# Products of loaded tiles by themselves in TensorE's waits, from Sinkhorn to v of batch 1

## The chip, the core and the metric

The kernel runs on one core of one Trainium2 chip. Its engines work side by side, each through its own list of instructions in order: TensorE (PE; its weight loads are listed as PEld), VectorE (DVE), ScalarE (ACT), GpSimd (POOL) and SyncE (SP), which here only issues DMAs. Sixteen DMA engines move data. The metric is the device time of one execution in microseconds (us); the profile comes from one further execution of the same program.

## What is computed

Sinkhorn attention over four batches of eight heads, 768 positions and 64 channels, followed by a token and channel mixer. Cut to what matters:

```python
# attention; q, k, v: (4, 8, 768, 64); sort_net: (4, 8, 8, 8)
P = sort_net
for _ in range(5):
    P = P - max(P, -1); P = exp(P)
    P = P / (sum(P, -1) + 1e-9)
    P = P / (sum(P, -2) + 1e-9)
k_sorted = einsum('bhij,bhjcd->bhicd', P, k_blocks)   # 8 blocks of 96 positions
v_sorted = einsum('bhij,bhjcd->bhicd', P, v_blocks)
attn = softmax(q_block @ k_sorted_block.T / 8)        # block by block
x = (attn @ v_sorted_block), heads beside each other: (4, 768, 512)
# mixer
u  = x + lam * einsum('ts,bsd->btd', w_tok, alpha1 * x + beta1)
a2 = alpha2 * u + beta2
out = u + lam * (relu(a2 @ w_ch1) @ w_ch2)            # 512 -> 2048 -> 512
```

## The kernel before

The order of the work is written out by hand: each engine gets its instructions in the order in which the Python code issues them, and the tile framework adds the semaphore waits. PSUM is held in two pools of two buffers each (`psS`, `psM`); `ps2` takes the next buffer of a pool, two banks of 512 columns.

The first 60 us, which the change touches, run in this order on TensorE.

1. While q and k of batch 0 arrive through GpSimd's DMA queue, 60 products of a column of ones by itself (L730) write to the tile `spare`. `sinkhorn` runs its five turns on VectorE and ScalarE with two yields a turn; between them `q_path(0)` transposes q of batch 0 on TensorE (L409) and ScalarE copies the result (L418).
2. `big_p("k")` spreads P over 128 partitions by a product (L258) and three VectorE operations (the last, L270, makes PTk). `mix_k(0)` mixes k of batch 0: three rounds of 64 small products (L309), each round into one buffer of each pool and copied out by ScalarE and VectorE (L294). `big_p(0)` does the same for v of batches 0 and 1.
3. `scores_max(0)` has eight steps, each with eight products (L447) and one maximum on VectorE (L453); between them go the eight steps of `mix_v(0)`, v of batch 0, each with eight products (L359) and a copy on ScalarE (L367).
4. `tok_weights` transposes w_tok (L685, six groups of six; copies L689, most of them on ScalarE), three groups ahead of `heads(0)` and three behind it. `heads(0)` computes, in eight steps, scores less their maxima (L490, L498), exponentials on ScalarE (L505), the products with v (L515) and the division on VectorE (L524, L525). After steps 4 and 8, `bounce` writes four blocks of x to DRAM on SyncE's queue (L535); at the end `read(0)` reads the first half back, on ScalarE's queue (L543), and `read(1)` the second, on SyncE's.
5. `row_sums` multiplies w_tok by ones (36 products of one column, L698), `big_p(1)` spreads P for batches 2 and 3, `mix_v(1)` makes v of batch 1 (L359, copies in turn on ScalarE and VectorE), with three VectorE additions (`add_x0`, L573) in between, and `mix_k(1)` mixes k of batch 1.
6. `mixing()` starts with `tok_mix(0)`: per group of 128 tokens, six products of 128x128 by 512 columns (L586). From there on the mixer's products (L586, L642, L664) and the attention of batches 1 to 3 are issued in turn by costs that the code counts.

GpSimd's queue loads, in order, q, k and v of batch 0, w_tok, v and k of batch 1, the small vectors, q of batch 1 and the first half of w_ch1 (W1); the second half of W1 and w_ch2 follow only when a copy on GpSimd (L778) has seen the second half of x of batch 0 read back.

Of the kernel before, what the change touches and what calls it, by code (L numbers as in the profile page):

```python
# [19 lines left out]
def kernel(  # L20
# [18 lines left out]
    nc = tc.nc  # L39
# [48 lines left out]
    raw_of = {}  # L88
# [194 lines left out]
            )  # L283


    kT_of, vS_of = {}, {}

    def kT_tile(b):
# [7 lines left out]
    def mix_k(b):  # L296

        raw, PK = raw_of["k", b], PT_of["k"]
        kT_tile(b)
        for rnd in range(3):  # L300
            ps = ps2(psM), ps2(psS)
            for turn in range(2):
                for tt in range(8):
                    for th in range(2):
                        for hl in range(2):
                            bank = (hl + turn) % 2
                            t = rnd * 16 + bank * 8 + tt
                            r = slice(th * 64 + hl * 32, th * 64 + hl * 32 + 32)
                            nc.tensor.matmul(  # L309
                                ps[th][hl * 64:hl * 64 + 64, bank, tt * 32:(tt + 1) * 32],  # L310
                                raw[r, t * D:(t + 1) * D], PK[r, b, hl * 32:hl * 32 + 32],
                                start=True, stop=True,
                            )
            for th in range(2):
                cols = ps[th][:, :, 0:256].rearrange("p b (t c) -> p c b t", c=32)
                evict_k(
                    b, cols, th * (BLK // 2) + rnd * 16,
                    nc.vector.tensor_copy if th else nc.scalar.copy,
                )
            yield 2.4  # L320
# [33 lines left out]
    def mix_v(b, pool):  # L354
        r = slice(b * 64, b * 64 + 64)
        for d8 in range(D // 8):
            ps = ps2(pool)
            for dd in range(8):
                nc.tensor.matmul(  # L359
                    ps[:, 0, dd * 64:(dd + 1) * 64],  # L360
                    v01[r].rearrange("p (t d) -> p d t", d=D)[:, d8 * 8 + dd, :],
                    PT_of[0][r, r], start=True, stop=True,
                )
            dst = vS_of[b][:, :, d8 * 8:(d8 + 1) * 8]
            src = ps[0:BLK, 0].rearrange("p (d c) -> p c d", c=64)
            if b == 0 or d8 % 2 == 0:
                nc.scalar.copy(dst, src)  # L367
            else:
                nc.vector.tensor_copy(dst, src)
            yield 1.1  # L370
# [66 lines left out]
    def scores_max(b):  # L437

        mx = at([BLK, 2, H4, NB], FT, "mx", 1)
        for n in range(2 * H4):  # L440
            h4, g = divmod(n, 2)
            sp = ps2(psS)
            for i1 in range(4):
                i = g * 4 + i1
                for hl in range(2):
                    r = slice(hl * 64, hl * 64 + 64)
                    nc.tensor.matmul(  # L447
                        sp[0:BLK, hl, i1 * BLK:(i1 + 1) * BLK],
                        qT_of[b, h4][r, i * BLK:(i + 1) * BLK],
                        kT_of[b][r, h4 * 8 + i, :],  # L450
                        start=True, stop=True,
                    )
            nc.vector.tensor_reduce(  # L453
                mx[:, :, h4, g * 4:(g + 1) * 4],
                sp[0:BLK, :, 0:4 * BLK].rearrange("p l (i t) -> p l i t", t=BLK),
                AXX, ALU.max,
            )
            yield 1.0


        mh = at([BLK, 2, 2, H4 * NB], BF, "mh", 1)
        mxf = mx[:].rearrange("p l h i -> p l (h i)")
        nc.vector.tensor_copy(mh[:, :, 0, :], mxf)
        nc.vector.tensor_tensor(mh[:, :, 1, :], mxf, mh[:, :, 0, :], ALU.subtract)
        yield END
        tp = psS.tile([128, 2, 1024], BF, name="m_ps", tag="psS")
        nc.tensor.transpose(
            tp[:, 0, 0:BLK], mh[:].rearrange("p l e c -> p (l e c)"), identbf[0:BLK, 0:BLK]
        )
        for g in range(2):  # L470
            Dt = D_of[b, g] = at([128, 4, BLK], BF, "Dt", 2)
            nc.vector.tensor_tensor(
                Dt[:], tp[:, 0, 0:BLK].unsqueeze(1).to_broadcast([128, 4, BLK]),
                mask_j[:, g * 4:(g + 1) * 4].unsqueeze(2).to_broadcast([128, 4, BLK]), ALU.mult,
            )
        yield END
# [3 lines left out]
    def heads(b, xpool):  # L480

        xnat = at([BLK, NB, C], F16, "xnat", 1)
        ETs = {}

        def scores(n):
            g, h4 = divmod(n, H4)
            sp = ps2(psS)
            for hl in range(2):
                r = slice(hl * 64, hl * 64 + 64)
                nc.tensor.matmul(  # L490
                    sp[0:BLK, hl, 0:4 * BLK], nsel[r, h4, :], D_of[b, g][r],
                    start=True, stop=False, skip_group_check=True,
                )
            for i1 in range(4):
                i = g * 4 + i1
                for hl in range(2):
                    r = slice(hl * 64, hl * 64 + 64)
                    nc.tensor.matmul(  # L498
                        sp[0:BLK, hl, i1 * BLK:(i1 + 1) * BLK],
                        kT_of[b][r, h4 * 8 + i, :],  # L500
                        qT_of[b, h4][r, i * BLK:(i + 1) * BLK],
                        start=False, stop=(i1 == 3), skip_group_check=True,
                    )
            ET = ETs[n] = at([BLK, 2, 4, BLK], F16, "ET", 3)
            nc.scalar.activation(  # L505
                ET[:].rearrange("p l i s -> p l (i s)"), sp[0:BLK, :, 0:4 * BLK],
                AF.Exp, scale=scale,
            )

        def values(n):  # L510
            g, h4 = divmod(n, H4)
            xp = ps2(xpool)
            for hl in range(2):
                for i1 in range(4):
                    nc.tensor.matmul(  # L515
                        xp[0:BLK, hl, i1 * VP:i1 * VP + D + 1],
                        ETs[n][:, hl, i1, :],
                        vS_of[b][:, hl * 32 + h4 * 8 + g * 4 + i1, 0:D + 1],
                        start=True, stop=True,
                    )  # L520
            xg = xp[0:BLK, :, 0:4 * VP].rearrange("p l (i e) -> p l i e", e=VP)
            recip = at([BLK, 2, 4], FT, "recip", 2)

            nc.vector.reciprocal(recip[:], xg[:, :, :, D])  # L524
            nc.vector.tensor_tensor(  # L525
                xnat[:, g * 4:(g + 1) * 4, :].rearrange(
                    "p i (l h d) -> p l i h d", l=2, d=D
                )[:, :, :, h4, :],
                xg[:, :, :, 0:D],
                recip[:].unsqueeze(3).to_broadcast([BLK, 2, 4, D]), ALU.mult,  # L530
            )

        def bounce(g):
            for i in range(g * 4, g * 4 + 4):
                nc.sync.dma_start(  # L535
                    xscr[b, i * BLK:(i + 1) * BLK].rearrange("(s k) c -> k s c", k=NT),
                    xnat[:, i],
                )

        def read(g):  # L540
            t0 = g * S // 2
            x16 = x16_of[b, g] = mt([128, NT // 2, C], F16, "x16", 2)
            (nc.scalar if b == 0 and g == 0 else nc.sync).dma_start(  # L543
                x16[:], xscr[b, t0:t0 + S // 2].rearrange("(kt p) c -> p kt c", p=128)
            )

        scores(0)
        yield 1.4
        for n in range(2 * H4):
            if n + 1 < 2 * H4:  # L550
                scores(n + 1)
            values(n)
            if n % H4 == H4 - 1:
                bounce(n // H4)
            if n == 2 * H4 - 1:
                read(0)
                read(1)
            yield 1.4
# [135 lines left out]
    def row_sums():  # L694
        ps = ps2(psM)
        for kt in range(NT):
            for ks in range(NT):
                nc.tensor.matmul(  # L698
                    ps[:, 0, kt:kt + 1], w_tokT[ks][:, kt * 128:(kt + 1) * 128], ones[:],
# [24 lines left out]
    for b in range(2):  # L724
        vS_tile(b)
    sink, q0 = sinkhorn(), q_path(0, psM)

    spare = ps2(psS)
    for _ in range(60):
        nc.tensor.matmul(spare[0:1, 0, 0:1], ones[:], ones[:], start=True, stop=True)  # L730
    for it in range(5):

        run(sink, 1)
# [2 lines left out]
        if it > 1:  # L736

            run(q0, 2)
        elif it == 1:
            run(q0, 1)  # L740
        if it == 0:
            spreads()

        run(sink, 1)
    run(q0)
    big_p("k")
    mk0 = mix_k(0)
    run(mk0, 1)
    big_p(0)
# [140 lines left out]
```

## Time and profile before

| | |
|---|---|
| time, median of 3 runs | 320.12 us (320.12 to 320.15) |
| time of the profiled execution | 319.92 us |
| its span, from the first to the last instruction | 317.5 us |
| PE busy | 295.0 us, 93% of the span, 3032 products |
| DVE, ACT, POOL busy | 155.3, 121.7 and 105.2 us |
| DMA | 31.78 MB, 100 GB/s over the span |
| first product of L586 | 58.06 us |

Times within the span are counted from its first instruction. A busy share is an average over stages with different limits: which stage the change touches, and what ends its waits there, has to be read from the trace. The span of a product is modelled, and those of neighbours overlap, so a pace is read from the starts of a run of products.

### The profile page before, as it was taken

The page shows a single profiled execution, that of the slowest core. Times are in us where ns is not written, and L with a number is a line of the kernel's source. Part 1 is how long each engine was busy: PE and PEld are TensorE (multiplying, and loading weights), DVE is VectorE, ACT ScalarE, POOL GpSimd, SP SyncE. Part 2 cuts the span into 40 slices and gives each one's busy share as a digit, 9 for nine tenths or more (in the row PEclk, how much of TensorE's full clock was granted, in tenths as well). Part 3 has the DMA queues.
Part 4 walks back from the last instruction along what each step waited for, and adds up shares of the span by engine and source line. Part 5 has one row for each costly group of instructions (what it writes and reads, how often), then busy time and mean ns, then how long its engine had stood idle before and what let it go on. Part 6 is the DMA issues. An engine that isn't in the chain of part 4 may idle for free.

```text
span 317.5 us, 6993 instructions
## 1 busy us (share of the span) xinstructions
PE 295.0 (93%) x3032; PEld 177.5 (56%) x3032; DVE 155.3 (49%) x287; ACT 121.7 (38%) x182; POOL 105.2 (33%) x107
## 2 busy tenths in 40 slices
PE   2689989999999899999999999999999999999994
PEld 2478878556555465444665466544545544554643
DVE  7576556597454355685457744631121342114123
ACT  4447433357832554422651065351503352330500
POOL 8313401777211451652101280643017482200000
PEclk9999999999999999999999999999999999999999
DMA  6999952998992549617114101131001000101001
GB/s 85 198 212 222 223 155 92 159 204 155 220 179 102 178 203 139 62 41 126 49 46 142 66 35 52 47 104 68 33 33 68 0 1 35 66 0 68 33 33 66
DMA packets 32270, 31.78 MB, mean 100 GB/s; under 512 B 13872, under 2 KB 27184, under 8 KB 31856
## 3 DMA queue, kind: packets, MB, share of 16 engines
q0 software_dynamic: 9632, 15.60, 27.8%
q1 hardware_dynamic: 22064, 15.22, 17.8%
q10 hardware_dynamic: 544, 0.52, 0.5%
q8 instruction: 23, 0.38, 0.5%
q14 instruction: 7, 0.06, 0.0%
HBM read 35.14 MB, written 11.01 MB: 145 GB/s over the span
## 4 chain that ended last, share of the span: by engine, by line
PE 80%; DVE 5%; ACT 5%; POOL 3%; DMA 3%; issue 2%; SPq 0%; ACTq 0%; DVEq 0%; POOLq 0%
PE psM L664 27%; PE psM L642 25%; PE psM L586 7%; PE psS L515 3%; PE psS L447 3%; POOL u L593 3%; PE psS L490 3%; PE q_ps L409 2%; PE psS L359 2%; DMA qn<-in_q_dram 2%; PE psS L498 2%; ACT ET L505 1%; PE psM L359 1%; DMA xscr<-xnat 1%; PE psM L515 1%
## 5 line engine op out<-in xcount | busy, mean ns | idle before, releaser
L642 PE MATMUL psM<-a2T,W 128*128 128x384 bf16 x512 | 89.1, 326 | 0.9 <-ACT hT L652 0.9
L664 PE MATMUL psM<-W,hT 128*128 128x512 bf16 (+1 forms) x400 | 87.2, 371 | 1.6 <-DVE tmp L671 0.9
L652 ACT ACTIVATE hT<-psM 128x768 bf16<-128x768 f32 x48 | 38.8, 810 | 83.7 <-PE psM L642 83.7
L642 PEld LDWEIGHTS <-W 128*128 128x128 bf16 x512 | 48.3, 98 | 32.4 <-issue 1.5
L664 PEld LDWEIGHTS <-hT 128*128 128x128 bf16 x400 | 37.9, 98 | 42.3 <-issue 2.6
L673 POOL TENSOR_TENSOR u<-u,tmp 128x512 f32<-128x512 f32 x18 | 22.7, 1262 | 87.7 <-DVE tmp L671 87.7
L593 POOL TENSOR_TENSOR u<-u,tmp 128x512 f32<-128x512 f32 x24 | 31.7, 1322 | 35.8 <-DVE tmp L592 24.3
L671 DVE TENSOR_TENSOR tmp<-psM,lamB 128x512 f32<-128x512 f32 (+1 forms) x25 | 16.8, 670 | 46.9 <-PE psM L664 46.0
L505 ACT ACTIVATE ET<-psS 96x768 f16<-96x768 f32 x32 | 25.5, 802 | 26.1 <-PE psS L498 26.0
L586 PE MATMUL psM<-x,w_tokT 128*128 128x512 f16 x144 | 35.2, 390 | 0.2 <-DVE tmp L592 0.2
L650 DVE TENSOR_SCALAR hT<-psM 128x768 bf16<-128x768 f32 x16 | 15.3, 956 | 39.2 <-PE psM L642 39.1
L453 DVE TENSOR_REDUCE mx<-psS 96x8 f32<-96x768 f32 x32 | 29.8, 949 | 6.0 <-PE psS L447 5.2
L592 DVE TENSOR_TENSOR tmp<-psM,a1lB 128x512 f32<-128x512 f32 x24 | 16.6, 690 | 12.9 <-PE psM L586 11.8
L586 PEld LDWEIGHTS <-w_tokT 128*128 128x128 f16 x144 | 13.3, 99 | 14.8 <-issue 1.4
L597 ACT CAST u<-u 128x512 bf16<-128x512 f32 x20 | 12.3, 617 | 20.6 <-POOL u L593 20.6
L568 POOL TENSOR_TENSOR u<-x,rb 128x1024 f32<-128x1024 f16 (+1 forms) x12 | 19.2, 1632 | 2.1 <-DMA x<-xscr 2.1
L515 PEld LDWEIGHTS <-ET 96*96 96x96 f16 x256 | 16.3, 140 | 4.1 <-ACT ET L505 2.1
L525 DVE TENSOR_TENSOR xnat<-psS,recip 96x512 f16<-96x512 f32 x24 | 16.5, 686 | 1.1 <-DVE recip L524 0.2
L524 DVE RECIPROCAL recip<-psS 96x8 f32<-96x8 f32 x24 | 4.9, 203 | 23.8 <-PE psS L515 23.5
L121 POOL DMA_DIRECT2D qn<-in_q_dram x16 | 11.6, 728 | 14.8 <-PE psM L359 5.4
L447 PE MATMUL psS<-kT,qT 64*96 64x96 f16 x256 | 13.9, 230 | 1.4 <-DVE kT L294 0.8
L447 PEld LDWEIGHTS <-qT 64*96 64x96 f16 x256 | 10.3, 134 | 8.2 <-issue 6.3
(105 smaller groups left out, 292.4 us busy)
## 6 DMA issues: line engine op xcount, KB each, us to landing
out_dram<-u SPq DMA_DIRECT2D x23, 256.0 KB
qn<-in_q_dram POOLq DMA_DIRECT2D x16, 192.0 KB, 7.0
raw<-in_k_dram POOLq DMA_DIRECT2D x8, 384.0 KB, 13.3
xscr<-xnat SPq DMA_DIRECT2D x32, 96.0 KB
x<-xscr SPq DMA_DIRECT2D x7, 384.0 KB
W<-in_moe_w_ch_dram POOLq DMA_DIRECT2D x2, 1024.0 KB, 10.0
W<-in_moe_w_ch_dram POOLq DMA_DIRECT2D x4, 512.0 KB, 12.6
v<-in_v_dram POOLq DMA_DIRECT2D x4, 384.0 KB, 15.0
```

Of the source, the lines that this page charges most:

```text
L447: nc.tensor.matmul(sp[0:BLK, hl, i1 * BLK:(i1 + 1) * BLK], qT_of[b, h4][r, i * BLK:(i + 1) * BLK], kT_of[b][r, h4 * 8 + i, :], start=True, ...
L453: nc.vector.tensor_reduce(mx[:, :, h4, g * 4:(g + 1) * 4], sp[0:BLK, :, 0:4 * BLK].rearrange("p l (i t) -> p l i t", t=BLK), AXX, ALU.max,)
L505: nc.scalar.activation(ET[:].rearrange("p l i s -> p l (i s)"), sp[0:BLK, :, 0:4 * BLK], AF.Exp, scale=scale,)
L515: nc.tensor.matmul(xp[0:BLK, hl, i1 * VP:i1 * VP + D + 1], ETs[n][:, hl, i1, :], vS_of[b][:, hl * 32 + h4 * 8 + g * 4 + i1, 0:D + 1], star ...
L568: nc.gpsimd.tensor_tensor(u_of[b][:, kt], x16_of[b, g][:, k0:k0 + kn], rb[:, kt], ALU.add)
L586: nc.tensor.matmul(ps[:, 0, :], w_tokT[ks][:, kt * 128:(kt + 1) * 128], x16_of[b, ks // 3][:, ks % 3, :], start=(ks == 0), stop=(ks == NT ...
L593: nc.gpsimd.tensor_tensor(u[:, kt], u[:, kt], tmp[:], ALU.add)
L642: nc.tensor.matmul(ps[:, m1, 0:384], W1[:, ci, m * 128:(m + 1) * 128], a2T_of[b, half, ci][:], start=(ci == 0), stop=(ci == CT - 1),)
L652: nc.scalar.activation(t_[:], ps[:, :, 0:384], AF.Relu)
L664: nc.tensor.matmul(ps[:, n, 0:c.stop - c.start], hT[m // 2][:, m % 2, k1 * 128:(k1 + 1) * 128], W2[:, m, c], start=(m == 0), stop=(m == HT ...
L671: nc.vector.tensor_tensor(tmp[:, c], ps[:, n, 0:c.stop - c.start], lamB[:, c], ALU.mult)
L673: eng.tensor_tensor(u[:, kt, c], u[:, kt, c], tmp[:, c], ALU.add)
```

## The change

A helper `busy(ps, src, n, cols)` issues n products of a tile's first 128 columns by its first `cols` columns into a PSUM buffer. Nothing reads what they write: the products that follow in the same place overwrite it, or it lies in columns or banks that are not used. The change issues such products

- before and during Sinkhorn, from q of batch 0 (16, then 4 and 12, then 8, of 128 columns each), while the 60 products of ones become 20, and 5 of 512 columns after `big_p("k")`,
- in each round of `mix_k`, from the tile of raw k: 2 of 512 columns ahead of the round and 2 of 256 in its middle. `mix_k` serves batches 0 and 1,
- in `scores_max(0)`, 3 of 512 ahead of the first step,
- in each step of `mix_v`, 1 of 512, for batches 0 and 1,
- in `heads(0)`, 2 of 512 ahead of the first step and 1 of 128 ahead of each of the others,
- in `row_sums`, 1 of 512 ahead of every second group.

`k_any` is assigned and not used.

```diff
--- before.py
+++ after.py
@@ -283,6 +283,12 @@
             )
 
 
+
+    def busy(ps, src, n, cols=512):
+        for _ in range(n):
+            nc.tensor.matmul(ps[:, 0:cols], src[:, 0:128], src[:, 0:cols], start=True, stop=True)
+
+
     kT_of, vS_of = {}, {}
 
     def kT_tile(b):
@@ -299,6 +305,7 @@
         kT_tile(b)
         for rnd in range(3):
             ps = ps2(psM), ps2(psS)
+            busy(ps[0][:, 0], raw, 2)
             for turn in range(2):
                 for tt in range(8):
                     for th in range(2):
@@ -311,6 +318,8 @@
                                 raw[r, t * D:(t + 1) * D], PK[r, b, hl * 32:hl * 32 + 32],
                                 start=True, stop=True,
                             )
+                if turn == 0:
+                    busy(ps[0][:, 0, 256:512], raw, 2, 256)
             for th in range(2):
                 cols = ps[th][:, :, 0:256].rearrange("p b (t c) -> p c b t", c=32)
                 evict_k(
@@ -355,6 +364,7 @@
         r = slice(b * 64, b * 64 + 64)
         for d8 in range(D // 8):
             ps = ps2(pool)
+            busy(ps[:, 1], raw_of["k", b], 1)
             for dd in range(8):
                 nc.tensor.matmul(
                     ps[:, 0, dd * 64:(dd + 1) * 64],
@@ -440,6 +450,8 @@
         for n in range(2 * H4):
             h4, g = divmod(n, 2)
             sp = ps2(psS)
+            if b == 0 and n == 0:
+                busy(sp[:, 0], raw_of["k", 0], 3)
             for i1 in range(4):
                 i = g * 4 + i1
                 for hl in range(2):
@@ -485,6 +497,8 @@
         def scores(n):
             g, h4 = divmod(n, H4)
             sp = ps2(psS)
+            if b == 0:
+                busy(sp[:, 0], raw_of["k", 0], *((1, 128) if n else (2,)))
             for hl in range(2):
                 r = slice(hl * 64, hl * 64 + 64)
                 nc.tensor.matmul(
@@ -694,6 +708,8 @@
     def row_sums():
         ps = ps2(psM)
         for kt in range(NT):
+            if kt % 2 == 0:
+                busy(ps[:, 1], raw_of["k", 1], 1)
             for ks in range(NT):
                 nc.tensor.matmul(
                     ps[:, 0, kt:kt + 1], w_tokT[ks][:, kt * 128:(kt + 1) * 128], ones[:],
@@ -724,10 +740,13 @@
     for b in range(2):
         vS_tile(b)
     sink, q0 = sinkhorn(), q_path(0, psM)
-
     spare = ps2(psS)
-    for _ in range(60):
+
+    for _ in range(20):
         nc.tensor.matmul(spare[0:1, 0, 0:1], ones[:], ones[:], start=True, stop=True)
+    q_any = qn_of[0, 0][:].rearrange("p l h k d -> p (l h k d)")
+    k_any = raw_of["k", 0]
+    busy(spare[:, 0], q_any, 16, 128)
     for it in range(5):
 
         run(sink, 1)
@@ -738,12 +757,16 @@
             run(q0, 2)
         elif it == 1:
             run(q0, 1)
+        if it > 1:
+            busy(spare[:, it % 2], q_any, (4, 12, 0)[it - 2], 128)
         if it == 0:
             spreads()
 
         run(sink, 1)
     run(q0)
+    busy(spare[:, 0], q_any, 8, 128)
     big_p("k")
+    busy(spare[:, 1], q_any, 5)
     mk0 = mix_k(0)
     run(mk0, 1)
     big_p(0)
```

## The prediction

> **What bounds the kernel now.** I read the page first: PE is busy 93% of a span of 317.5 us, and token and channel mixing (L586, L642, L664) carry the chain's end. The change touches only the 58 us before token mixing, so what counts is when the first L586 starts, and at what pace. Next, single lines of the program, for the price of one product early and late (minimum/median/maximum in ns):
>
> ```profile
> L515 PE MATMUL psM<-vS,ET x64: 268/268/290, 31.8 to 42.9; 96*96 96x65 f16 x64
> L515 PE MATMUL psS<-vS,ET x192: 195/210/231, 84.3 to 200.2; 96*96 96x65 f16 x192
> L586 PE MATMUL psM<-x,w_tokT x3: 606/634/634, 58.1 to 58.9; 128*128 128x512 f16 x3
> L586 PE MATMUL psM<-x,w_tokT x140: 376/379/634, 59.7 to 259.4; 128*128 128x512 f16 x140
> ```
>
> The same products cost much more before about 60 us than after. By pace the step is nearly two: eight L515 take 0.78 us early and 0.48 late, six L586 take 2.67 and then 1.40. The page's clock row hides this:
>
> ```profile
> PEclk9999999999999999999999999999999999999999
> ```
>
> It shows full speed throughout, but the trace's clock records begin only at 60.78 us (full, for 256.0 us; then half, from 316.78). So TensorE runs its first 60 us at half clock, and 2.7 us of dense L586 (58.06 to 60.78) raise it. The last product ends at 313.9; 2.9 us later the clock is half again.
>
> Then the chain of waits in 0 to 60 us, in order of time (start, length):
>
> ```profile
> 40.01 0.70 SPq L535
> 40.75 4.10 DMA xscr<-xnat
> 44.95 0.39 ACTq L543
> 45.38 0.81 ACT w_tokT L689
> 46.23 1.10 PE psM L698 x36
> 47.33 0.16 PE psS L258
> 47.49 3.20 PE psS L359 x32
> ```
>
> The row sums (L698) do not wait for TensorE. Half of batch 0's x is written to DRAM (L535); the read-back on ScalarE's queue (L543) waits for that write, and a copy of w_tokT that the row sums need stands behind it. Why the write takes until 44.85 is in the windows of the DMA engines (last columns: DMA share, GB/s):
>
> ```profile
> 40.00:41.00 1.00, 1.00 (x15) 0.82 (x15) 0.40 (x2) 0.66 (x1) 0.00 (x0) 1.00 1.16 219
> ...
> 44.00:45.00 1.00, 0.84 (x9) 0.84 (x10) 0.57 (x2) 0.00 (x0) 0.00 (x0) 1.00 0.11 34
> ```
>
> GpSimd's loads run at some 205 GB/s from 3 to 41 us; the last, half of W1, moves from 36.4. The write's first issue ends at 39.2, yet its first packet moves at 41.12, as that load drains; with the engines free (issue end 44.83) it came 0.6 us after.
>
> **The change, part by part.** Dummies, priced as full-array products. Half clock: 512 columns 0.445 us (2.67/6), 256 half of it, 128 columns 0.108 (six L685 in 0.65). Full clock: 512 columns 0.233 or less (1.40/6; in longer runs of L664, 0.216), 128 columns 0.065 (12 L613 in 0.78).
>
> Up to k mixing. Forty tiny products go: nothing, as TensorE then waits for q until 4.98 and again until 7.92. The first 16 dummies (1.7 us) lie in that second wait, 4 more (0.43) in the gap 9.41 to 10.06. The 12 (1.3) put the last q transposes at 12.1 to 12.9, and the 8 (0.86) end at 13.8, 0.7 after L258's present start. Then 5 of 512 run beside VectorE's PTk chain, and 2 more ahead of the first k product. At half clock that product starts 2.9 us later; if the clock has risen by 13 us, about 0.7. Sinkhorn itself doesn't move: ScalarE's exponentials don't stand behind the later transposes.
>
> Does the clock rise? I weigh each product's columns by the share of the 128x128 array that it fills. Heads (half clock, 1.58 us a step) come to 0.45, scores with v to 0.40 to 0.47, and 24 us of these never raised it; the window from 57.4 that did held 0.82. From 9.4 to 17 us the new stream holds about 0.73 without its transposes, and above 0.8 in its last 4 us; k mixing, at half clock, 0.67. I take it to rise between 13 and 20 us.
>
> K mixing, per round: 2 of 512 and 2 of 256, 0.66 us at full clock, part of it in round two's wait for an eviction. Scores of batch 0 start about 1.3 us later (0.5 to 2.3). Three dummies fit their wait of 0.79 for kT. Scores with v then go by VectorE's maxima (0.95 each), TensorE needing about 0.25 + 0.22 + 0.45; some 0.7 is won back. Heads fall from 1.58 to about 1.02 a step (0.48 for L515, 0.47 for L490 with L498, 0.065), so they end near 40.1, not 43.1, and the w_tokT transposes near 42.0 instead of 45.6.
>
> Where that gain goes: nowhere. The first write of x is now issued from about 36.4, still behind the W1 load, so it lands near 44.85 as before, and the row sums start at 46.2. TensorE waits 4.2 us. In the trace 2.9 us without products cost it the clock, so it begins the row sums at half clock, with dummies on its path:
> - row sums: 1.10 + 3 x 0.445 = 2.44, to 48.7; L258, 48.9
> - v of batch 1 (L359): eight groups of 0.80 (100 ns each, TensorE busy throughout), now each + 0.445: 9.96, to 58.8. Its density is (0.445 + 0.22)/1.245 = 0.53, little above what never raised the clock
> - k mixing of batch 1: rounds of 1.0 + 1.33. Density 0.67 raises the clock after some 3.5 us (one and a half rounds), the rest at 1.66: 6.0, to 64.8
> - first L586 group at full clock: 1.40, to 66.2.
>
> Before, that group ended at 60.73: +5.5. Nothing later changes: x is in place by 52, and W1 and W2 are requested two us earlier, not later. If the clock rises only with L586, as today: 58.8 + 7.0 + 2.67 = 68.5, +7.7. The profiled execution took 319.92 (2.4 beyond its span); its time with 5.5 more is 325.4, and the median lies 0.2 above it: 325.6.
>
> A rule beside this: the Trainium skill (TensorE: Matmul & The Clock Gate, Part 1: The HAM clock gate) says that the clock is half or full by what the array did in a free-running window of 3.4 us, and that one idle window halves it. The trace's two steps agree (2.7 us of dense work, 2.9 idle); by the rule a wait of 4.2 us need not hold a whole window, which would leave a chance that the clock holds. The page's Part 4 says that transposes don't count as activity. By it, TensorE is idle from 40.1, and the clock is lost for sure.
>
> **Rivals.**
> - The clock holds through the wait. For: nothing in the trace says how little work is enough, and the window from 88.1 held it at 0.46; the w_tokT transposes shorten the empty stretch. Then row sums 1.8, L258 0.2, v 8 x 0.69 (VectorE's eviction decides), k mixing 3.6 to 5.0 (its real products 0.55 to 1.0 a round: the trace has them only at half clock), L586 1.40: 58.7 to 60.1, so 0.6 to 2.0 faster, 318.1 to 319.5.
> - The clock is lost and is back by 51.4, within v, if 0.53 is enough: 51.4 + 6 x 0.69 + 3.6 to 5.0 + 1.40 = 60.5 to 61.9: 319.9 to 321.3.
> - Faster: the write of x is not held up. If the queues share, or its first issue comes before W1's packets (36.4, that is 1.3 us sooner than I reckon), it lands 3.6 us after its last issue (as 47.1 to 50.7 did), at 42.9; row sums start at 44.2, the wait is 2 us, the clock holds, and 2.0 is added to the first rival: 316.1 to 317.5. Against: no packet of it moved from 39.8 to 41.1 while W1 did. It decides from a landing before 43.5. The skill's DMA: Bandwidth & Descriptors (Queues, rings and completion order) has each engine take turns between its queues by whole packets; that speaks for this rival, and the trace's 1.3 us without a turn against it.
> - The change doesn't do what it says: the threshold lies above what it reaches, and the clock never rises early. Then 2.9 + 0.4 + 0.8 + 1.3 in k mixing, 0.6 + 8 x 0.445 with the maxima, 1.6 in heads, 11 in all, less 0.6 of slack, then up to 8: 331 to 339.
>
> **Numbers.** Forecast (clock lost, back only in k mixing or later) 0.45, its own range 324.5 to 328.5; back within v 0.18; held 0.18; write not held up 0.10; never raised 0.09. A measurement here tells apart about 0.2%, 0.64 us. Faster by more: 0.16 of the held case, the unheld write, 0.03 of the third: 0.29. Same: 0.02 + 0.05 = 0.07. Slower: 0.45 + 0.09 + 0.10 = 0.64. The range 317.5 to 328.5 leaves out the unheld write and the never-raised case, 0.19.
>
> **What would show it.** Products on PE rise from 3032 to about 3092 (60 - 20 fewer, 100 more). Early L515 at about 210 ns and heads' steps near 1.0 us: the clock was up. L698 still near 46.2, behind L543 at 44.95: the write decides. L359 of batch 1 at 270 ns and L586's first group near 65: forecast right. I am wrong if L698 starts before 45, if its wait is under 2 us, or if L359 of batch 1 runs at the late price.

## The result, and the profile after

| | before | after |
|---|---|---|
| median of 4 runs each | 320.13 us (320.12 to 320.35) | 334.87 us (332.03 to 336.61) |
| ratio, 95% interval | | 1.045 [1.0365, 1.0535] |
| profiled execution, its span | 319.92, 317.5 | 336.61, 334.8 |
| products on PE | 3032 | 3092 |
| clock records, full from | 60.78 us | 12.85 to 26.50, then from 77.70 us |

Slower, as forecast, but by some 15 us where 5.5 were expected, and outside the range. The profiled execution is the longest of the four and has the lowest mean granted clock: 0.922 of full speed, against 0.938 to 0.948 in the other three.

The lines of the changed kernel have moved down by 10 to 23: the dummies are L289, v's products L369 (were L359), the maxima's scores L459 (L447), heads L504, L512, L529 (L490, L498, L515), the row sums L714 (L698), token mixing L600 (L586).

The page's clock row of the changed kernel (each digit a slice of 8.4 us) now shows what the row before could not, since a record begins early (ahead of that record, up to 12.85 us, it still shows full speed):

```profile
PEclk9995555558999999999999999999999999999999
```

The windows of the changed kernel, cut at those records (length; busy time with instructions of PE, PEld, DVE, ACT, POOL; clock, DMA share, GB/s):

```profile
12.85:26.50 13.65, 13.05 (x294) 8.33 (x292) 7.37 (x13) 4.20 (x7) 2.75 (x6) 1.00 1.09 212
26.50:77.70 51.20, 49.70 (x580) 32.91 (x579) 22.61 (x41) 16.59 (x24) 10.52 (x14) 0.50 0.72 144
```

The dummies did raise the clock, ahead of k mixing. It fell again at 26.50, in the middle of the maxima, although TensorE had been busy for 13.05 of the 13.65 us before, and stayed down for 51 us. So no long wait took it. Early L529 shows the same, with the old half-clock median of 268 ns where 210 was the sign of a raised clock:

```profile
L529 PE MATMUL psM<-vS,ET x64: 268/268/287, 39.5 to 51.2; 96*96 96x65 f16 x64
```

The chain of waits of the changed kernel in the maxima (start, length, what), one step at full clock and one at half:

```profile
25.32 0.20 PE psS L459 x5
25.52 0.32 PE psM L289
25.85 0.84 PE psM L369 x8
26.68 0.35 PE psS L459 x6
27.04 0.54 PE psM L289
27.58 0.68 PE psM L369 x6
```

The first of these steps takes 1.36 us, from 25.32 to 26.68, at full clock: 0.84 of it are v's eight products. The next takes 1.75 (26.68 to 28.43). VectorE waits. In the kernel before it set the pace, as its timeline there shows, with five maxima in a row and no gap:

```profile
23.02 4.95 DVE L453 TENSOR_REDUCE mx<-psS 96x8 f32<-96x768 f32 x5 [0.43 <-PE psS L447]
```

And from the end of heads to token mixing:

```profile
52.51 0.83 PE wT_ps L699 x6
53.37 0.81 ACT w_tokT L703
54.22 0.59 PE psM L289
...
57.30 0.85 PE psS L369 x8
...
67.92 0.97 PE psM L289 x2
...
75.69 2.41 PE psM L600 x6
```

The copy of w_tokT now waits for its transposes (L699), which end at 53.34; the read-back L557 had been issued at 52.09 and held nothing up. About nine tenths of the chain from 20 to 78 us are TensorE's own work.

| start, us | before | after | forecast |
|---|---|---|---|
| first product of the maxima | 19.01 | 20.51 | 20.3 |
| last maximum (end) | 27.97 | 33.33 | |
| first product of heads | 30.00 | 37.66 | |
| last product of heads' L515/L529 | 42.87 | 51.23 | heads end 40.1 |
| row sums, dummy included | 46.23 | 54.22 | 46.2 |
| first group of token mixing (end) | 60.73 | 78.10 | 66.2 |

The differences add up to the span's 17.3: 1.5 to the maxima, 3.9 in them, 2.3 from there to heads, 0.7 in heads, 0.4 back before the row sums (together 8.0), then 23.9 us instead of 14.5 from the row sums to the end of the first group (9.4). From there on both kernels run alike.

### The profile page after: what moved, and what is told of

Same layout as the page of the kernel before. It is cut to its first block, busy times and chain, and to the rows that moved or that the text cites. A ratio compares the mean times of both kernels' runs of the same rounds, so it can differ in the third digit from the quotient of the medians.

```text
span 334.8 us, 7114 instructions
## 1 busy us (share of the span) xinstructions
PE 318.8 (95%) x3092; PEld 185.0 (55%) x3092; DVE 156.8 (47%) x287; ACT 122.0 (36%) x182; POOL 105.1 (31%) x107
## 4 chain that ended last, share of the span: by engine, by line
PE 85%; DVE 4%; ACT 4%; POOL 3%; DMA 2%; issue 1%; DVEq 0%; POOLq 0%; ACTq 0%
PE psM L678 25%; PE psM L656 24%; PE psM L600 7%; PE psM L289 3%; PE psS L504 3%; PE psS L529 3%; PE psS L289 3%; PE psS L459 3%; POOL u L607 3%; PE psS L369 2%; PE q_ps L419 2%; PE psS L512 2%; PE psM L369 2%; DMA qn<-in_q_dram 2%; PE psM L529 2%; ACT ET L519 1%
## 5 line engine op out<-in xcount | busy, mean ns | idle before, releaser
L600 PE MATMUL psM<-x,w_tokT 128*128 128x512 f16 x144 | 35.0, 388 | 0.2 <-DVE tmp L606 0.2
L600 PEld LDWEIGHTS <-w_tokT 128*128 128x128 f16 x144 | 13.3, 99 | 14.8 <-issue 1.4
L529 PEld LDWEIGHTS <-ET 96*96 96x96 f16 x256 | 16.3, 140 | 3.7 <-ACT ET L519 1.7
L369 PEld LDWEIGHTS <-v 64*128 64x128 f16 x128 | 12.8, 206 | 6.7 <-issue 6.7
L459 PEld LDWEIGHTS <-qT 64*96 64x96 f16 x256 | 10.1, 127 | 7.6 <-issue 6.0
```

What stands on the lines that cost most here:

```text
L369: nc.tensor.matmul(ps[:, 0, dd * 64:(dd + 1) * 64], v01[r].rearrange("p (t d) -> p d t", d=D)[:, d8 * 8 + dd, :], PT_of[0][r, r], start=Tr ...
L459: nc.tensor.matmul(sp[0:BLK, hl, i1 * BLK:(i1 + 1) * BLK], qT_of[b, h4][r, i * BLK:(i + 1) * BLK], kT_of[b][r, h4 * 8 + i, :], start=True, ...
L529: nc.tensor.matmul(xp[0:BLK, hl, i1 * VP:i1 * VP + D + 1], ETs[n][:, hl, i1, :], vS_of[b][:, hl * 32 + h4 * 8 + g * 4 + i1, 0:D + 1], star ...
L600: nc.tensor.matmul(ps[:, 0, :], w_tokT[ks][:, kt * 128:(kt + 1) * 128], x16_of[b, ks // 3][:, ks % 3, :], start=(ks == 0), stop=(ks == NT ...
```

## The experiments

Kernels sent together shared a chip and its runs of the kernel before. On the later chips those runs alone lay between 319.1 and 325.3, so each ratio is against its own neighbours. In 20 of these 42 runs the mean granted clock was 0.938 to 0.978, where the profile of the kernel before has 0.999. In the kernel with the queue alone (below) 0.973 goes with a clock that rose at 34.46, so in these 20 it probably came up early too, with no dummy; that is argued, not shown.

### Batch 1's dummies left out, and batch 1's alone

First, the changed kernel without the dummies in the row sums, in v and in k mixing of batch 1:

```diff
-            busy(ps[0][:, 0], raw, 2)
+            if b == 0:
+                busy(ps[0][:, 0], raw, 2)
...
-            busy(ps[:, 1], raw_of["k", b], 1)
+            if b == 0:
+                busy(ps[:, 1], raw_of["k", b], 1)
...
-            if kt % 2 == 0:
-                busy(ps[:, 1], raw_of["k", 1], 1)
```

> The changed kernel without the dummies for batch 1 (row sums, v and k mixing of batch 1). Theory A (the clock is lost while the maxima and v of batch 0 run, and from there each dummy is paid at half clock on TensorE's path): the stretch from the first row-sum product to the end of the first token-mixing group goes back from 23.9 us to the 14.5 of the kernel before, so 9.4 us come back: about 325.5 us, with the row sums still starting near 54 us. Theory B (the late start alone is the loss: x is read back late and token mixing waits for it, so that the dummies behind the row sums lie in that wait): token mixing still starts near 75, 333 to 335 us.

Measured 323.38 us, ratio 1.0043 [0.9994, 1.0092]; profiled 320.88. Its chain of waits:

```profile
47.51 0.81 ACT w_tokT L705
48.35 1.10 PE psM L714 x36
...
59.46 2.67 PE psM L602 x6
```

Row sums to the first group's end: 62.13 - 48.35 = 13.8 us, against 23.9 with the dummies. In this profile the clock was lost at 25.06, in the maxima again, but came back at 35.30, and heads ran in steps of 1.01 us, the forecast's 1.02. It fell again at 45.54. The wait of the row sums for the write of x (landed 46.98), the read-back and the copy came after that, from 46.97 to 48.35; so the clock was lost ahead of the row sums, as forecast, but not by this wait.

Up to the row sums this program is the changed kernel. There they started at 54.22, here at 48.35, where 54 had been expected: the maxima started 1.0 us earlier, GpSimd's products came too late to collide with VectorE (below), and the clock came back ahead of heads. So the delay of 8.0 us ahead of the row sums belongs to the profiled execution, and is not a fixed price of these dummies.

Second, the kernel before with nothing but these dummies:

```diff
+            if b == 1:
+                busy(ps[0][:, 0], raw, 2)
...
+                if turn == 0 and b == 1:
+                    busy(ps[0][:, 0, 256:512], raw, 2, 256)
...
+            if b == 1:
+                busy(ps[:, 1], raw_of["k", b], 1)
...
+            if kt % 2 == 0:
+                busy(ps[:, 1], raw_of["k", 1], 1)
```

> The kernel before with the dummies for batch 1 alone. Theory A (they are paid in full at half clock; their density does not raise it): row sums at 46.2 us as before, then 23.9 instead of 14.5 us: about 329.5 us. Theory B (the clock rises within v or k mixing of batch 1, so that part of it is won back, as the prediction had it): 325 to 327 us.

Measured 329.66, ratio 1.0294 [1.0201, 1.0387]; profiled 329.4. Its chain of waits:

```profile
46.58 0.59 PE psM L288
...
49.12 0.54 PE psS L288
49.66 0.86 PE psS L370 x8
...
68.06 2.67 PE psM L597 x6
```

From 46.58 to 70.73: 24.2 us, close to the changed kernel's 23.9, and the clock rises only at 70.99. So these dummies stand wholly on TensorE's path, at the half-clock price, and never raise the clock themselves: the larger part of the loss, and independent of what came before. The same ratio on the 320.13 us beside the changed kernel gives an estimate of 329.5 (326.6 to 332.5 by its interval): these dummies alone bring the time to the upper end of the forecast's range.

### V's dummies of batch 0, or all after k mixing, left out

```diff
-            busy(ps[:, 1], raw_of["k", b], 1)
+            if b == 1:
+                busy(ps[:, 1], raw_of["k", b], 1)
```

> The changed kernel without the dummies in v of batch 0. Theory A (they lie on the path: eight products of v take 0.83 us at either clock, so a step is theirs plus the scores' plus the dummy's, not the maximum's 0.95): maxima's steps back to 1.0 us, and VectorE's two operations behind the maxima no longer collide with GpSimd's products; row sums start 4 to 6 us sooner, 329 to 331 us. Theory B (they hold the clock up to 26.5 us and pay for themselves): the clock is lost one window sooner and the time is 334 us or more.

Measured 329.37, ratio 1.0263 [1.0177, 1.0349]; profiled 330.84. Steps of the maxima are back at 1.0, the clock is lost there too (22.39), comes back at 32.63, heads step by 1.0, and the row sums' first dummy starts at 47.1, right behind the copy that waits for x. Then 24.1 us to the first group's end at 71.27. With eight dummies less, 7.1 of the 8.0 us of delay ahead of the row sums are gone. Part of that is that the clock came back, which it did with these dummies too in the kernel without batch 1's. What is left is 10.5 at the first group's end: the forecast's other branch, in which k mixing doesn't raise the clock (7.7), a gate 0.9 later, and 1.9 for batch 1's groups and rounds, which cost more than reckoned (below).

The next one keeps the dummies up to k mixing of batch 0 and drops every one behind it, those in v, maxima, heads, row sums and batch 1:

```diff
-            busy(ps[0][:, 0], raw, 2)
+            if b == 0:
+                busy(ps[0][:, 0], raw, 2)
...
-            busy(ps[:, 1], raw_of["k", b], 1)
...
-            if b == 0 and n == 0:
-                busy(sp[:, 0], raw_of["k", 0], 3)
...
-            if b == 0:
-                busy(sp[:, 0], raw_of["k", 0], *((1, 128) if n else (2,)))
...
-            if kt % 2 == 0:
-                busy(ps[:, 1], raw_of["k", 1], 1)
```

> The changed kernel with only the dummies up to k mixing of batch 0; none with the maxima, v, heads, row sums or batch 1. Theory A: the clock rises near 13 us, the maxima start 1.5 us later than before, the clock is lost by 24 us, and 0.6 us of slack is there: 320.5 to 321.5 us. Theory B (the clock, once up, holds through maxima and heads by their own products): heads at about 1.0 us a step, row sums near 46.2 or earlier, 318 to 319.5 us.

Measured 321.75, ratio 0.9984 [0.9944, 1.0025]: no difference. The clock is full from 10.66 to 20.90, and its maxima start at 20.23, 1.2 later than before; by the row sums (47.07) the delay is 0.8. So the part up to k mixing costs next to nothing, and brings nothing.

### V's weights read from adjacent elements

Eight products of 64 columns take 0.84 us at full clock and 0.85 at half. Something other than the array's clock sets them. Their stationary operand steps by 64 elements, 128 bytes; this kernel takes 128 adjacent elements instead, and so mixes v from other elements than the reference does:

```diff
-                    v01[r].rearrange("p (t d) -> p d t", d=D)[:, d8 * 8 + dd, :],
+                    v01[r, (d8 * 8 + dd) * 128:(d8 * 8 + dd + 1) * 128],
```

> The changed kernel with v's products (both batches) reading 128 neighbouring columns of the v tile as weights, not columns 128 bytes apart; so v is mixed from the wrong elements, and the output is not the reference's. Theory A (v's products take 0.10 us each at either clock because their weights are read with a stride): at full clock eight of them take 0.4 to 0.55 us instead of 0.83, a maxima step with its dummy about 1.0 to 1.1 us instead of 1.35, and the maxima end 2 us or more sooner. Theory B (the clock or the small size sets their pace): 0.83 us as before.

Measured 328.16 (one run; 319.92 for the kernel before beside it). Its line L369 (minimum/median/maximum in ns), after the same line of the changed kernel:

```profile
L369 PEld LDWEIGHTS <-v x128: 160/211/233, 21.1 to 67.6; 64*128 64x128 f16 x128
L369 PE MATMUL psM<-PT,v x64: 186/271/300, 21.1 to 33.5; 64*128 64x64 f16 x64
```

```profile
L369 PEld LDWEIGHTS <-v x128: 92/98/128, 23.1 to 57.9; 64*128 64x128 f16 x128
L369 PE MATMUL psM<-PT,v x64: 190/190/200, 23.1 to 30.2; 64*128 64x64 f16 x64
```

and its maxima on VectorE's timeline (start, length):

```profile
25.50 5.28 DVE L465 TENSOR_REDUCE mx<-psS 96x8 f32<-96x768 f32 x6 [0.77 <-PE psS L459]
```

The median weight load falls from 211 to 98 ns. By clock, it was 211 at full and 208 to 212 at half with the step, and from adjacent elements 95 at full and 128 at half. Six maxima follow each other without a gap in 5.28 us, and the clock is full from 16.21 to 43.52, through maxima and heads. The row sums start at 47.00, right behind the copy that waits for x; the first group ends at 68.61. That is 7.9 behind the kernel before, and 8.2 in time, next to the forecast's other branch of 7.7. That closeness is partly luck: a group of v of batch 1 takes 1.08 us here, less than the 1.245 of that branch, while the gate is 0.8 later and k mixing of batch 1 takes 7.77 and not 7.0. But v's price at full clock is set by the strided weights, and without it the clock was held through the maxima.

### GpSimd's two products moved to VectorE, behind heads

After the last maximum two small VectorE operations took 1.9 us instead of 0.4. The timeline of the changed kernel, VectorE and GpSimd:

```profile
33.37 0.64 DVE L475 CAST mh<-mx 96x64 bf16<-96x64 f32 x1
34.04 1.24 DVE L476 TENSOR_TENSOR mh<-mx,mh 96x64 bf16<-96x64 f32 x1
```

```profile
33.93 1.27 POOL L779 TENSOR_TENSOR b1lB<-tmp,lamB 128x512 f32<-128x512 f32 x1
```

In the kernel before, VectorE's two operations ran at 28.00 and 28.23, ahead of GpSimd's products (L756 there, from 32.97).

```diff
-    for dst, src in ((a1lB, alB), (b1lB, blB)):
-        nc.gpsimd.tensor_tensor(dst[:], src[:], lamB[:], ALU.mult)
...
     run(heads(0, psM))
+    for dst, src in ((a1lB, alB), (b1lB, blB)):
+        nc.vector.tensor_tensor(dst[:], src[:], lamB[:], ALU.mult)
```

> The changed kernel with the two products a1lB and b1lB on VectorE behind heads, not on GpSimd while the maxima end. Theory A (VectorE's two small operations behind the maxima took 0.64 and 1.24 us instead of 0.19 and 0.22 because GpSimd's two products ran at the same time): they take 0.19 and 0.22 us, and heads start about 1.4 us sooner after the last maximum. Theory B (the slow clock or TensorE's state did it): they stay at 0.6 us or more.

Measured 335.21 (one run). VectorE's timeline:

```profile
33.29 0.19 DVE L475 CAST mh<-mx 96x64 bf16<-96x64 f32 x1
33.52 0.22 DVE L476 TENSOR_TENSOR mh<-mx,mh 96x64 bf16<-96x64 f32 x1
```

The two operations have their old price, and heads start 3.5 us behind the last maximum instead of 4.3: 0.8 sooner, not the expected 1.4. The collision is shown; in time it is worth less than the spread of the runs.

This profile shows more. Its clock fell at 26.22 in the maxima and came back at 36.46, and heads ran in steps of 1.0 us. Their last product started at 45.59, 5.6 us ahead of the changed kernel's, yet the first dummy of the row sums started at 51.59, only 2.6 ahead. Between them stands the write of x, whose last issue for the first half ended at 45.80 and which landed at 49.61:

```profile
45.11 4.50 DMA xscr<-xnat
```

So when heads end late, a faster clock in heads is half swallowed by the same gate.

### More dummies in the maxima and heads

If density holds the clock, a denser stream should keep it: three dummies of 512 columns in each step of v for batch 0, one of 512 in each step of heads, none in batch 1.

```diff
...
-            busy(ps[:, 1], raw_of["k", b], 1)
+            if b == 0:
+                busy(ps[:, 1], raw_of["k", b], 3)
...
-                busy(sp[:, 0], raw_of["k", 0], *((1, 128) if n else (2,)))
+                busy(sp[:, 0], raw_of["k", 0], *((1,) if n else (2,)))
...
```

> The changed kernel with three dummies of 512 columns in each maxima step instead of one, one of 512 in each step of heads instead of 128 columns, and none for batch 1. Theory A (the clock holds while a window's work fills more than about a third of the array, and dummies are paid in full): clock full from about 13 us to the end of heads without a break, maxima steps about 1.85 us, heads about 1.2 us, row sums near 52, 325 to 328 us. Theory B (the clock is lost for another reason than the density, such as the short wait for instructions in the second step): a break at half clock within the maxima all the same.

Measured 332.94 (one run). The clock was lost at 26.35 all the same, but the chain shows a stall in the 3.4 us ahead of it, in which TensorE waited for nothing that the profile shows:

```profile
22.87 1.83 issue
24.70 0.81 PE psM L289 x3
```

With it that stretch is no denser than the others that lost the clock (0.25, by the prediction's measure). So this run doesn't tell whether a dense stream without stalls holds the clock. It does show the price: 2.6 us a step once the clock is gone. And it shows that density by this measure doesn't raise the clock by itself: at half clock the maxima came to 0.61 to 0.78, and the clock rose only at 46.83.

### Dummies up to k mixing, with the maxima's first three and in heads

```diff
-            busy(ps[0][:, 0], raw, 2)
+            if b == 0:
+                busy(ps[0][:, 0], raw, 2)
...
-            busy(ps[:, 1], raw_of["k", b], 1)
...
-            if kt % 2 == 0:
-                busy(ps[:, 1], raw_of["k", 1], 1)
```

> The changed kernel without the dummies in v of both batches, in the row sums and in k mixing of batch 1: what is left raises the clock ahead of Sinkhorn's end and again, with the transposes of w_tok, ahead of heads. Theory A (the write of x gates the row sums through ScalarE's queue): heads at about 1.0 us a step end near 42, the row sums still start at 46 to 47.5 behind the read-back's issue, 320 to 321.5 us. Theory B (TensorE alone sets the row sums' start): they start at 44 to 45, 317.5 to 318.5 us.

Measured 319.66, ratio 0.9942 [0.9902, 0.9982]; profiled 318.34. Heads run at full clock, in steps of 1.0 us, and their last product starts at 41.07, near the forecast's 40.1. Its chain of waits:

```profile
40.60 4.23 DMA xscr<-xnat
44.92 0.39 ACTq L557
45.35 0.81 ACT w_tokT L703
46.20 1.10 PE psM L712 x36
```

The row sums start at 46.20 (before 46.23). This is the forecast's gate to a tenth: heads 1.8 us earlier, and none of it gets through.

### The first read-back on SyncE's queue

The same kernel with the gate taken away: the copy of w_tokT no longer stands behind the read-back.

```diff
-            (nc.scalar if b == 0 and g == 0 else nc.sync).dma_start(
+            nc.sync.dma_start(
```

> The same kernel with the first read-back of x issued on SyncE's queue, so that no copy of w_tokT stands behind it. Theory A: the row sums start at 44 to 45 us, 2 to 3 us sooner than with the read-back on ScalarE's queue, 317.5 to 319 us. Theory B (the queue does not matter): the time of the kernel with the read-back on ScalarE, within 0.3 us.

Measured 317.94, ratio 0.9898 [0.9853, 0.9943]; profiled 317.5. Its chain of waits:

```profile
42.55 1.41 PE wT_ps L699 x12
43.99 0.57 DVE w_tokT L703
44.60 0.98 PE psM L712 x31
```

The row sums follow their transposes (the first at 44.20, 2.0 us sooner than with the read-back on ScalarE's queue), and the first group of token mixing ends at 58.32, 2.4 us ahead of the kernel before. This version beats the kernel before and the changed kernel. Its clock fell at 42.66 although no wait of TensorE's between heads and the row sums is longer than 0.52 us.

Two more take it apart: heads' dummies and the queue on the kernel before, and the queue alone.

```diff
...
+            if b == 0:
+                busy(sp[:, 0], raw_of["k", 0], *((1, 128) if n else (2,)))
...
-            (nc.scalar if b == 0 and g == 0 else nc.sync).dma_start(
+            nc.sync.dma_start(
```

> The kernel before with the dummies of heads alone (2 of 512 columns ahead, 1 of 128 a step) and the first read-back on SyncE's queue. Theory A (two dummies and the w_tok transposes fill a window enough to raise the clock where its phase is lucky): heads partly at 1.0 us a step, row sums at 43 to 46, 316.5 to 320 us by the phase. Theory B (without the early dummies the clock does not rise before heads): heads at 1.69 a step, row sums near 48, 321 to 322 us.

Measured 320.16 (315.69 to 320.72), ratio 0.9892 [0.9817, 0.9968].

```diff
-            (nc.scalar if b == 0 and g == 0 else nc.sync).dma_start(
+            nc.sync.dma_start(
```

> The kernel before with only the first read-back of x moved to SyncE's queue. Theory A: the copy of w_tokT no longer waits for the write, but at half clock the transposes of w_tok end at 45.6, so the row sums start near 46: at most 0.4 us faster than before. Theory B (the write costs more than that): 1 us or more faster.

Measured 319.33 (316.6 to 325.42), ratio 0.9924 [0.9888, 0.9961]. The three intervals overlap: that the queue gains is shown (by the ratio about 2.4 us, more than the expected 0.4), that dummies add to it is not. In its profile the clock rose at 34.46 with no dummy in the program, and k mixing holds a stall:

```profile
16.23 3.10 issue
```

The one with heads' dummies has such a stall too, 3.04 us at 16.39. Both profiles thus start the maxima 2.4 us later than the kernel before, and run heads at full clock. That such stalls and the moment at which the clock rises make the spread of these runs is argued from two profiles, not shown.

## Why the prediction was wrong, and where it was right

**Right, with their numbers.** TensorE runs its first 60 us at half clock, in the profile on which the forecast rests; the early dummies raise it (12.85 us, and 8.0 to 16.2 in the other kernels that have them; forecast 13 to 20); k mixing delays the maxima by 1.5 (1.3); heads at full clock step by 1.0 to 1.01 (1.02); the gate at the row sums stands at 46.2 when heads end early, and taking the read-back out of ScalarE's queue opens it; the clock is gone when the row sums start; batch 1's dummies are paid in full at half clock; a few dense products of token mixing raise it.

**Right by luck.** The forecast lost the clock in TensorE's wait ahead of the row sums. It fell before that wait: at 42.87 in the kernel without v's dummies (wait from 44.06), at 45.54 without batch 1's (46.97), at 42.48 with the dummies up to k mixing and in heads (43.63), and at 42.66 where the queue had taken the wait away. What the four have in common ahead of it is a thin stretch, the end of heads and the last transposes, of 0.28 to 0.31 by the prediction's measure.

**The step that failed** is "Scores with v then go by VectorE's maxima (0.95 each), TensorE needing about 0.25 + 0.22 + 0.45". V's eight products measured 0.83 to 0.86 at full clock, the dummy 0.32 and the scores 0.20 of the chain: 1.36, and TensorE became the bound. The 0.45 is about half of the 0.80 to 0.85 that these products take at half clock, as if the clock set their price; the strided weight load sets it, at either clock. The same products in a longer step are a thinner stream: 0.30 by the prediction's measure in the 3.4 us ahead of 26.50, where the clock fell; at 0.95 a step it would have been 0.30 x 1.36/0.95 = 0.43, and at that measure no run lost it. Two later steps fell with it in the profiled execution: "Heads fall from 1.58 to about 1.02 a step" (1.69: the half-clock price and a dummy of 0.108), and the row sums at 46.2 (54.22). This is 8.0 of the 11.9 us between the forecast's 5.5 and the span's 17.4 at the first group's end. How much of the 8.0 comes, though, hangs on whether the clock returns ahead of heads: with the same maxima it did at 35.30 without batch 1's dummies and at 36.46 with VectorE's products, and the row sums stood 2.1 and 5.4 us behind 46.2. What decides it is open. With contiguous weights all three came out close to what was written (0.88, 1.0, 47.0).

**The terms that were mis-sized** make the other 3.9. A v group of batch 1 took 1.395, not 1.245: a dummy between small products costs 0.54, not 0.445, and the products 0.85, not 0.80 (1.2 us in eight). K mixing of batch 1 took 7.77, not 6.0, and the first group 2.41, not 1.40, because k mixing, at 0.46 to 0.71 by its measure, did not raise the clock (2.8); in the kernel with batch 1's dummies alone it did not either. The branch "only with L586" was the right one, and had the lesser weight in the sum.

**Not foreseen**: the collision of VectorE and GpSimd (1.5 us of VectorE's time, 0.8 at the start of heads), only because the maxima slipped past 32.6. The Trainium skill (SBUF — State Buffer, SBUF: two separate sides) says that a VectorE operation with two SBUF inputs and a GpSimd operation that reads SBUF exclude each other for a whole instruction. The trace agrees: L476 took 1.24 us beside L779 and 0.22 without.

**The rivals.** The time lies in the range of "never raised", 331 to 339, yet that rival's condition was false. Its sum came close since it priced the same dummies at half clock. "The write is not held up" was not borne out: with heads ending 1.8 us earlier it landed at 44.83, as before. Whether W1's load or the later issues hold it was not separated; with VectorE's products, W1's load had ended at 43.6, and the write still landed 3.8 us after its last issue (45.80 to 49.61), so that load isn't needed for so long a wait. Nor does it keep the write from starting: with batch 1's dummies alone the first packet moved at 40.51, 0.6 us after the first issue had ended, while the load ran on to 42.1.

**What stays open** is how little work holds the clock, and how much raises it. Every record of these runs but the last, which ends with the trace, is a multiple of 3.413 us long (13.65 is 4 of them, 51.2 is 15, 256 is 75). By the prediction's measure, an estimate from columns and array share over such stretches, the clock was lost at 0.25 to 0.32 and held at 0.33 and more, but once also at 0.29 (from 19.39 with VectorE's products). It rose at 0.64 to 1.00, but not at 0.72 in the stretch of the kernel before from 26.65, nor at 0.76 and 0.78 with more dummies (from 26.35 and 36.6). So this measure alone doesn't tell when it rises. The Trainium skill (TensorE: Matmul & The Clock Gate, Part 1: The HAM clock gate) gives a window of that length and lets the clock fall after an idle one: the length agrees, but the stretches that lost it were not idle, a quarter to a third full.

## What to carry to other kernels

Before a product is priced at another clock, see what sets it now: if the same eight take as long at both, something else sets it (here a strided weight load), and filling around it lengthens the step. Work added to keep a clock up is paid in full wherever the engine has no wait, so look for the wait in each stage first, and for the gate behind it that would swallow the gain. Here one queue for one transfer gained as much as could be shown for any set of dummies that was tried.

## What the runs showed of the hardware

- A weight load of 64 rows by 128 columns took about 211 ns at either clock with a step of 128 bytes. From adjacent elements it took 95 ns at full clock and 128 at half.
- Transposes seem to help to raise the clock. In the kernel with the queue alone and no dummy it rose at 34.46; of the 0.71 in the 3.4 us ahead, thirteen w_tokT transposes make 0.41 (13 x 128 of 4096 columns at half clock), and the other 0.30 is less than the 0.45 at which heads never raised it, and than the 0.78 without a transpose that did not raise it either. Alone they did not do it: in the same profile q's transposes came to 0.67 from 7.2 to 10.6, with nothing beside them, and the clock stayed at half. The Trainium skill (TensorE: Matmul & The Clock Gate, Part 4: PE-mode transpose) has it that they don't count as busy in the same way; this measurement, an estimate by one measure, speaks against their counting for nothing.
- The clock fell without a wait: in a stretch in which PE was busy for 3.25 of 3.42 us by the profile (23.08 to 26.50), so PE's busy share alone is no measure of what holds it.
- TensorE stood for 1.83, 3.04 and 3.10 us in three of the profiles with nothing shown that it waited for, while the DMA engines were full (a share of 1.12 to 1.15). The DMA records point to its instructions: each of the three, and seven shorter ones of 0.25 to 0.90 us in eight profiles in all, ended 1.3 to 1.5 us after a transfer on the queue that the page lists as "instruction" had ended (17.89 and 19.34, for instance, with the queue alone). That was not tried.
